# Gathering two heads in six moves, mixing and rounding on ScalarE, and a new order: a fused attention and gated feed-forward kernel

## The chip, the cores and the metric

The kernel runs on one core of one Trainium2 chip. The metric is device time in microseconds (us) of one execution. Engines are called PE (TensorE, the matrix engine), DVE (VectorE), ACT (ScalarE), POOL (GpSimd) and SP (SyncE, which issues the DMAs here).

## The reference

Inputs are q, k, v and a complex decay a of shape (4 batches, 8 heads, 768 steps, 48), and weights for a feed-forward part. In attention each head keeps a complex 48x48 state that is multiplied by the decay at every step and takes up one outer product:

```python
mag = np.sqrt(a_re * a_re + a_im * a_im)
scale = np.minimum(mag, 0.999) / (mag + 1e-06)
for t in range(S):
    new_re = ar * S_re - ai * S_im
    new_im = ar * S_im + ai * S_re
    S_re, S_im = (new_re + kv, new_im)          # kv = outer(k_t, v_t)
    y[:, :, t] = np.einsum('bhd,bhde->bhe', q[:, :, t], S_re)
```

The result, x of shape (4, 768, 384), goes through the feed-forward part:

```python
xk = mu_k * x + (1.0 - mu_k) * x_prev           # x_prev: x one step earlier
xr = mu_r * x + (1.0 - mu_r) * x_prev
k = np.maximum(xk @ w_k, 0.0)
v = k * k @ w_v                                 # 384 -> 1024 -> 384
return 1.0 / (1.0 + np.exp(-(xr @ w_r))) * v
```

## The kernel before

**Units.** The work is cut into eight units of 384 steps (half a batch each), numbered u. A unit has three parts. `gate(u)` loads q, k and a into the tile g (three column tiles ct of 128 rows), takes logarithms and angles of the decay (Ln, Exp, Arctan on ACT, prefix sums by scans on DVE), and multiplies k and q by growth and phase, which leaves cosine and sine products in g (line 777, six instructions in unit 0, two long ones later). `attend(u)` makes the attention from them: transposes `tr` of the keys, copies `kt` by ACT, state increments `up`, scores `sc`, masks `pt` by DVE, states added up by DVE, and values `y`. `mix(u)` is the feed-forward part: mixed inputs x, first products `z`, relu r, square h, second products `o`.

**Heads in pairs.** A column tile ct holds two heads in rows 0 to 47 and 64 to 111, and 16 rows of heads 6 and 7 in rows 48 to 63 and 112 to 127 of each of the three tiles. So heads 0 to 5 (pairs 0 to 2) can be scored from g as it lies, and heads 6 and 7 (pair 3) can't: their parts must be brought together by DMA. Line 806 (`move` in `stack`) does that for pair 3 with 12 moves of 16 rows, cosine and sine apart, into the tile q23. It also moves the queries of pairs 0 to 2 into the tiles q01 and q23, four moves for each pair, for the product with the state. For pair 3 both q and k go, and its scores are taken from q23 (line 986) and not from g (line 991).

**Unit 0 of the feed-forward part** uses whole fp32 weights (`wx`) and inputs; each block of weights comes as 64-bit numbers (`raw`, ten loads, 768 KB each and one of 384 KB) and is converted by ACT (line 583) and DVE (lines 586, 589, 593). From unit 1 on the weights are split into a rounded high part and a rest (`split`, lines 613 and 616), and so are x (lines 418 and 421) and h (hhi by a cast of line 495, hlo by a subtraction of line 499); every product is then three fp32r multiplications. Unit 0's x is one difference dx on DVE (line 395) and two fused multiply-adds (line 404) for each ct; it needs the rows of pair 3 back in place, which six DMAs xt<-ys do (line 1079).

**Order.** Everything is recorded as operations with reads, writes and buffer slots. A planner (`Plan.run`) plays them through with estimated costs, picking on each engine the ready operation with the lowest number of the table `ORDER`, and then emits the instructions in that order. `ORDER` holds a number for each engine of each step: "g" gate, "f" load of weights, "w" conversion, "a" attention, "m" feed-forward, "s" split. Engines run their own queues in order and wait for each other by semaphores. A DMA takes one of eight semaphores in turn, and waits until the DMA that had it eight issues earlier has landed; so at most eight are in flight from SP.

**Loads.** Those of unit 0's and unit 1's g (12 of 384 KB), the weights, and v (192 KB each) all go out from SP in the first 25 us, in the order that the table gives.

Of the kernel before, what the change touches and what calls it, by code (L numbers as in the profile page):

```python
# [22 lines left out]
P = 128  # L23
# [29 lines left out]
    ("g", 4): dict(SP=(69, 89, 43, 39, 47, 54,), ACT=(170, 75, 186, 162, 178,), DVE=(196, 188, 101, 194, 213,)),
    ("g", 5): dict(SP=(103, 102, 100, 97, 71, 81,), ACT=(148, 217, 190, 204, 206,), DVE=(154, 209, 211, 189, 172,)),
    ("g", 6): dict(SP=(105, 91, 109, 30, 107, 104,), ACT=(198, 153, 133, 211, 141,), DVE=(191, 71, 208, 179, 205,)),
    ("g", 7): dict(SP=(98, 93, 96, 94, 90, 99,), ACT=(183, 164, 201, 205, 215,), DVE=(167, 160, 171, 169, 150,)),
    ("f", 0): dict(SP=(16,)),
    ("f", 1): dict(SP=(35,)),
    ("f", 2): dict(SP=(15,)),
    ("f", 3): dict(SP=(14,)),  # L60
    ("f", 4): dict(SP=(65,)),
    ("f", 5): dict(SP=(73,)),
    ("f", 6): dict(SP=(101,)),
    ("f", 7): dict(SP=(75,)),
    ("f", 8): dict(SP=(40,)),
    ("f", 9): dict(SP=(72,)),
    ("w", 0): dict(ACT=(63,), DVE=(164,)),
    ("w", 1): dict(ACT=(120,), DVE=(142,)),
    ("w", 2): dict(ACT=(91,), DVE=(121,)),
    ("w", 3): dict(ACT=(8,), DVE=(20,)),  # L70
    ("w", 4): dict(ACT=(173,), DVE=(214,)),
    ("w", 5): dict(ACT=(60,), DVE=(138,)),
    ("w", 6): dict(ACT=(43,), DVE=(98,)),
    ("w", 7): dict(ACT=(13,), DVE=(31,)),
    ("w", 8): dict(ACT=(104,), DVE=(68,)),
    ("w", 9): dict(ACT=(9,), DVE=(56,)),
    ("a", 0): dict(DVE=(5, 6, 60, 46, 45, 42, 8, 43, 19,), SP=(12, 45, 5, 28, 83,), PE=(3, 28, 32, 4, 19, 6, 8, 31, 9,
         13, 0, 5,), ACT=(4, 122, 3, 146, 37, 20, 61,), POOL=(0,)),
    ("a", 1): dict(SP=(31, 6, 23,), PE=(23, 7, 2, 1, 39, 11, 15,), DVE=(7, 2, 9, 15, 35, 13,), ACT=(89, 23, 52, 92,
         56,)),  # L80
    ("a", 2): dict(SP=(58, 22, 34,), PE=(102, 79, 70, 92, 119, 140, 108,), DVE=(30, 85, 36, 75, 112, 137,), ACT=(35,
         114, 107, 31, 22,), POOL=(3,)),
    ("a", 3): dict(SP=(11, 67, 20,), PE=(20, 33, 52, 89, 59, 68, 43,), DVE=(44, 135, 22, 32, 161, 28,), ACT=(163, 157,
         177, 175, 62,)),
    ("a", 4): dict(SP=(80, 52, 49,), PE=(65, 170, 180, 95, 22, 93, 85,), DVE=(147, 61, 190, 50, 78, 118,), ACT=(145,
         207, 187, 195, 191,), POOL=(2,)),
    ("a", 5): dict(SP=(42, 50, 63,), PE=(124, 86, 134, 49, 66, 130, 72,), DVE=(113, 153, 134, 139, 202, 141,), ACT=(185,
         155, 152, 174, 137,)),
    ("a", 6): dict(SP=(77, 92, 84,), PE=(144, 152, 178, 179, 169, 131, 129,), DVE=(170, 183, 173, 184, 168, 193,),
         ACT=(169, 189, 159, 172, 144,), POOL=(1,)),  # L90
# [7 lines left out]
    ("m", 2): dict(DVE=(97, 23, 109, 119, 105, 86, 16, 73, 62, 29, 80, 76, 11, 37,), ACT=(67, 73, 83, 109, 93, 108, 101,
         105, 33, 119, 97, 112, 95, 124, 82,), PE=(42, 91, 16, 77, 138, 17, 14, 84, 67, 40, 99, 88, 90, 94, 24, 53, 87, 27,
         78,), SP=(74, 64, 68,)),  # L100
    ("m", 3): dict(DVE=(81, 74, 82, 132, 92, 99, 122, 47, 131, 140, 69, 91, 149, 84,), ACT=(29, 84, 30, 72, 80, 111,
# [1148 lines left out]
```

## Time and profile before

| | |
|---|---|
| three runs | 440.93, 439.72, 437.56 us; median 439.72 |
| the profiled execution | 439.72 us; its span, first to last instruction, 438.0 us |
| mean granted PE clock | 0.961 of full speed |
| PE busy | 376.4 us (86%) |
| DVE, ACT busy | 341.4 us (78%), 308.6 us (70%) |
| DMA over the span | 49.72 MB |

The rest of a run beside the span, 1.7 us, lies before the first and after the last instruction. The profile counts an instruction as busy from its start to its end; neighbours on an engine overlap a little, and matmuls overlap much. A share over the whole span says little here, since the start of the program has other limits than its middle, so the stages are read one by one.

### The profile page before, as it was taken

The numbers are of one execution on the slowest core, as the hardware profiler recorded it, in microseconds if no ns is written. First come the engines' busy times: TensorE is split into PE (matmuls) and PEld (weight loads), VectorE is DVE, ScalarE is ACT, GpSimd is POOL, SyncE is SP. The second block draws the span as 40 slices with busy tenths as digits, with TensorE's granted clock in tenths as the row PEclk, the third lists the DMA queues.
The fourth block names the chain that finished last, engine by engine and source line by source line (L and its number), as shares of the span: only waits on it lengthen the run. The fifth ranks groups of instructions, "written<-read, shape, count | busy, mean of one in ns | idle before, by whom it ended". The sixth has DMA issues, their size and how long they took to land.

```text
span 438.0 us, 13423 instructions
## 1 busy us (share of the span) xinstructions
PE 376.4 (86%) x5681; PEld 336.4 (77%) x5681; DVE 341.4 (78%) x564; ACT 308.6 (70%) x595; POOL 7.1 (2%) x30
## 2 busy tenths in 40 slices
PE   0027735999997999899999999999999999999994
PEld 0016622666576998899989999999989999999993
DVE  0998789999986889978898998979998873527232
ACT  6878385978895679876995799669968741534430
POOL 4000000000000000000000000000000000000000
PEclk9998585999998999999999999999999999999998
DMA  7996270326134513404542724164210341001001
GB/s 276 415 413 165 57 258 27 75 66 257 29 75 120 217 50 81 104 30 182 148 94 72 269 49 90 55 257 112 56 57 10 80 100 57 16 0 54 2 1 62
DMA packets 23189, 49.72 MB, mean 114 GB/s; under 512 B 4945, under 2 KB 16465, under 8 KB 23121
## 3 DMA queue, kind: packets, MB, share of 16 engines
q1 hardware_dynamic: 23120, 48.78, 35.7%
q8 instruction: 47, 0.77, 0.7%
q14 instruction: 22, 0.17, 0.1%
HBM read 31.07 MB, written 4.72 MB: 82 GB/s over the span
## 4 chain that ended last, share of the span: by engine, by line
PE 60%; DVE 14%; ACT 11%; DMA 6%; issue 4%; SPq 3%; DVEq 0%; ACTq 0%
PE z L443 23%; PE o L520 17%; PE y L1028 8%; PE up L877 4%; PE sc L991 3%; SPq L806 3%; DMA q<-g 2%; DMA xt<-ys 2%; PE tr L848 2%; DVE g L777 2%; PE sc L986 2%; DVE m L715 2%; ACT sq L317 1%; PE z L439 1%; DMA v<-in_vt 1%
## 5 line engine op out<-in xcount | busy, mean ns | idle before, releaser
L443 PE MATMUL z<-x,w 128*128 128x384 f32 x693 | 132.4, 340 | 0.0
L443 PEld LDWEIGHTS z<-x,w 128*128 128x128 f32 x693 | 119.3, 188 | 1.4
L520 PE MATMUL o<-hhi,w 128*128 128x384 f32 x336 | 87.6, 342 | 0.3 <-DVE hhi L495 0.3
L520 PEld LDWEIGHTS o<-hhi,w 128*128 128x128 f32 x336 | 59.4, 188 | 1.5 <-DVE hhi L495 0.8
L520 PE MATMUL o<-hlo,w 128*128 128x384 f32 x168 | 57.0, 339 | 0.6 <-DVE hlo L499 0.6
L484 ACT ACTIVATE r<-z 128x384 f32<-128x384 f32 x64 | 31.0, 487 | 35.4 <-PE z L443 33.2
L495 DVE CAST hhi<-h 128x384 fp32r<-128x384 f32 x56 | 19.3, 354 | 34.9 <-ACT h L488 21.9
L777 DVE TENSOR_TENSOR g<-g,r 128x768 f32<-128x768 f32 (+1 forms) x24 | 41.3, 1755 | 4.9 <-ACT r L317 4.5
L439 PE MATMUL z<-x,wx 128*128 128x384 f32 x66 | 25.5, 533 | 12.9 <-DVE x L404 12.9
L317 ACT ACTIVATE sq<-m 128x1152 f32<-128x1152 f32 (+1 forms) x30 | 28.1, 966 | 9.9 <-DVE m L698 6.1
L488 ACT ACTIVATE h<-r 128x384 f32<-128x384 f32 x64 | 33.0, 526 | 0.9
L520 PEld LDWEIGHTS o<-hlo,w 128*128 128x128 f32 x168 | 31.6, 188 | 2.2 <-DVE hlo L499 2.1
L499 DVE TENSOR_TENSOR hlo<-h,hhi 128x384 fp32r<-128x384 f32 x56 | 30.4, 553 | 1.5
L908 PE MATMUL tr<-ident,g 128*128 128x128 f32 x18 | 3.6, 335 | 32.5 <-DVE g L777 30.7
L439 PEld LDWEIGHTS z<-x,wx 128*128 128x128 f32 x66 | 13.0, 206 | 22.1 <-issue 11.9
L1028 PEld LDWEIGHTS y<-q,state 112*48 112x48 f32 (+1 forms) x704 | 24.2, 138 | 7.1 <-issue 5.3
L1028 PE MATMUL y<-q,state 112*48 112x64 f32 (+1 forms) x704 | 27.1, 233 | 2.5 <-PE up L947 0.8
L314 ACT ACT_TABLE_LOAD x22 | 28.2, 1283 | 0.4
L418 ACT CAST x<-xm 128x384 fp32r<-128x384 f32 x42 | 21.0, 513 | 9.8 <-DVE xm L410 4.9
L908 PEld LDWEIGHTS tr<-ident,g 128*128 128x128 f32 x18 | 2.3, 165 | 33.2 <-issue 29.8
L1003 DVE TENSOR_TENSOR pt<-sc,mask 128x384 f32<-128x384 f32 (+1 forms) x36 | 17.0, 507 | 13.2 <-PE sc L986 8.4
L877 PEld LDWEIGHTS up<-v,kt 64*64 64x64 f32 (+1 forms) x1216 | 21.4, 127 | 7.2 <-issue 2.8
(88 smaller groups left out, 663.1 us busy)
## 6 DMA issues: line engine op xcount, KB each, us to landing
g<-in_gat SPq DMA_DIRECT2D x18, 768.0 KB, 5.8
raw<-in_w_all SPq DMA_DIRECT2D x9, 768.0 KB, 10.5
g<-in_gat SPq DMA_DIRECT2D x12, 384.0 KB, 7.9
v<-in_vt SPq DMA_DIRECT2D x24, 192.0 KB, 3.6
q<-g SPq DMA_DIRECT2D x96, 48.0 KB, 2.2
out_t<-y SPq DMA_DIRECT2D x24, 192.0 KB, 2.3
q<-g SPq DMA_DIRECT2D x28, 144.0 KB, 3.3
q<-g SPq DMA_DIRECT2D x40, 72.0 KB, 2.8
```

Of the source, the lines that this page charges most:

```text
L314: nc.scalar.add_instruction(mybir.InstLoadActFuncSet(name=nc.get_next_instruction_name(), act_func_set_id=loaded[0], engine=mybir.EngineTy ...
L317: nc.scalar.activation(out=out, in_=in_, func=func, **kw)
L418: nc.scalar.copy(out=hi[which][:, ct], in_=xm[which, ct])
L439: nc.tensor.matmul(z, lhsT=wx[s[0]][:, s[1]], rhs=hi[which][:, ct], start=ct == 0, stop=ct == NT - 1)
L443: nc.tensor.matmul(z, lhsT=wt[s[0]][:, part, s[1]], rhs=r[which][:, ct], start=n == 0, stop=n == 3 * NT - 1)
L484: nc.scalar.activation(out=t["r", j], in_=t["f", j], func=AF.Relu, scale=1.0 / W_SCALE)
L488: nc.scalar.activation(out=t["h", j], in_=t["r", j], func=AF.Square)
L499: nc.vector.tensor_tensor(out=t["lo", j], in0=t["h", j], in1=t["hi", j].bitcast(F32), op=ALU.subtract)
L520: nc.tensor.matmul(tiles["o", mt], lhsT=w, rhs=r, start=j == 0 and n == 0, stop=j == NJ - 1 and n == len(parts) - 1)
L777: nc.vector.tensor_tensor(out=g[:, d, 2 * i:2 * i + 2], in0=g[:, d, 2:4], in1=t["r"][:, 1 - i, d].unsqueeze(2).to_broadcast([P, k, 2, U]), ...
L877: nc.tensor.matmul(t["up", c, s][i * HR:(KR if i else HR), h * D:(h + 1) * D], lhsT=keys, rhs=V[u][c][r, h * D:(h + 1) * D], start=True, s ...
L1028: nc.tensor.matmul(t["y", team][s][rows, h // 2 - team[0], c], lhsT=lhsT[:, cols], rhs=rhs, start=(s, h % 2) not in begun, stop=stop)
```

## The change

- *Heads 6 and 7 of unit 0.* Instead of 12 moves of 16x768 into q23, six moves of 16x1536 (all four rows: cosine and sine of k and q at once) bring them into a tile g67 that is laid out like g. Their scores are computed from it like those of the other pairs, with 24 multiplications instead of 12 of twice the depth. Four copies on ACT then put the queries into q23.
- *Mixed input of unit 0.* ACT writes (1 - mu) times the earlier step, DVE adds mu times x in one fused operation; the difference dx is gone there. A tile mu_1 of 1 - mu is made once.
- *Rounded h.* In units 1 to 3, for every second block j, hhi is a Square of relu on ACT and no longer a cast on DVE.
- *Prologue of unit 0.* The Relu of two of the three column tiles goes to DVE (`RELU_0`), and ACT's table set 6 is loaded ahead of everything.
- *First state of each pair in unit 0.* Copied by ACT, no longer by DVE.
- *Planner.* It now knows that at most eight DMAs are in flight (`LANES`), and starts with the table "exp" loaded. All of `ORDER` is new; two of its lines stand here for all.

```diff
 ORDER = {
-    ("g", 0): dict(SP=(7, 8, 1, 10, 13, 9, 3, 2, 0,), ACT=(36, 14, 6, 27, 25, 19, 39, 28, 41, 40, 5, 11, 18, 42, 1,),
+    ("g", 0): dict(SP=(4, 20, 11, 35, 10, 21, 22, 103, 29,), ACT=(88, 48, 54, 156, 91, 218, 166, 175, 65, 197, 223, 118,
...
-HHI_ACT = set()
+HHI_ACT = {(u, j) for u in (1, 2, 3) for j in range(1, NJ, 2)}
+RELU_0 = (1, 2)
...
+    LANES = 8
...
-        table, dma, end = None, 0.0, 0.0
+        table, dma, end = "exp", 0.0, 0.0
...
+                    if e == "SP" and len(lanes) >= self.LANES and lanes[-self.LANES] + self.LATENCY > t:
+                        continue
...
+    mu_1 = keep.tile([P, 2, NT], F32, name="mu_1")
+    nc.vector.tensor_scalar(out=mu_1, in0=mu_sb, scalar1=-1.0, scalar2=1.0, op0=ALU.mult, op1=ALU.add)
...
-                def whole_one(which=which):
+                def whole_old(which=which):
                     if which not in hi:
                         hi[which] = mp["x"].tile([P, NT, 2, U], F32R, tag=("xk", "xr")[which], name="x")[:, :, 0].bitcast(F32)
+                    nc.scalar.activation(out=hi[which][:, ct], in_=X[u][:, ct, 0:U], func=AF.Copy,
+                                         scale=mu_1[:, which, ct:ct + 1])
+
+                def whole_new(which=which):
                     nc.vector.scalar_tensor_tensor(
-                        out=hi[which][:, ct], in0=d[ct], scalar=mu_sb[:, which, ct:ct + 1],
-                        in1=X[u][:, ct, 0:U], op0=ALU.mult, op1=ALU.add)
+                        out=hi[which][:, ct], in0=X[u][:, ct, 1:U + 1], scalar=mu_sb[:, which, ct:ct + 1],
+                        in1=hi[which][:, ct], op0=ALU.mult, op1=ALU.add)
...
-                if j in HHI_ACT:
-                    nc.scalar.activation(out=t["hi", j], in_=t["h", j], func=AF.Copy)
+                if (u, j) in HHI_ACT:
+                    nc.scalar.activation(out=t["hi", j], in_=t["r", j], func=AF.Square)
...
+            if (u, j) in HHI_ACT:
+                op_act(U, h_hi, reads=[("rl", u, j)], writes=[("hhi", u, j)], uses=[sr, s1])
+            else:
+                op_dve(U, h_hi, rate=2, reads=[("h", u, j)], writes=[("hhi", u, j)], uses=[sh, s1])
...
+                if u == 0 and c.start in RELU_0:
+                    op_dve(n, positive_dve, rate=2, reads=gk(c, 0), writes=kk("m", c), uses=[s_ph, s_m, s_g])
...
+                    def gather(ct, j):
+                        if "g67" not in t:
+                            t["g67"] = mp["x"].tile([P, 2 * NT, U], F32, tag="xr", name="g67")[:, :4]
+                        o = j * HR + 16 * ct
+                        nc.sync.dma_start(out=t["g67"][o:o + 16], in_=G[u][j * HR + D:j * HR + HR, ct])
+
+                    def copy(i, j):
+                        nc.scalar.copy(out=qs[1][i * HR:i * HR + D, j, 2], in_=t["g67"][j * HR:j * HR + D, 2 * i + 1])
...
-                            nc.vector.tensor_copy(new, t["up", p, s][:, c])
+                            nc.scalar.copy(out=new, in_=t["up", p, s][:, c])
...
-                                    if p == NT:
+                                    if p == NT and u:
...
-                                    g = G[u][j * HR:j * HR + D, p]
+                                    g = G[u][j * HR:j * HR + D, p] if p < NT else t["g67"][j * HR:j * HR + D]
...
         with tc.manual_schedule():
+            load_table(6)
             plan[0].run(ORDER)
```

The instructions' order changes on every engine. Three places of it matter in what follows. SP's queue around unit 0's moves stood thus before (`q_92` is q01 and `q_93` is q23; `xt<-ys` brings heads 6 and 7 back into x):

```order
L806 DMA q_92<-g 48x384 x2
L806 DMA q_93<-g 48x384 x2
L806 DMA q_92<-g 48x384 x2
L806 DMA q_93<-g 48x384 x2
L806 DMA q_93<-g 16x768 x12
L806 DMA q_92<-g 48x384 x4
L636 DMA g<-in_gat 128x1536 x3
L1079 DMA xt<-ys 16x384 x2
L643 DMA v<-in_vt 128x384 x3
L1079 DMA xt<-ys 16x384 x4
```

and stands thus now (`g_408` is g67):

```order
L585 DMA raw<-in_w_all 128x1536
L662 DMA v<-in_vt 128x384 x3
L832 DMA q_92<-g 48x384 x4
L832 DMA q_93<-g 48x384 x4
L832 DMA q_92<-g 48x384 x4
L850 DMA g_408<-g 16x1536 x6
L655 DMA g<-in_gat 128x1536 x3
L1131 DMA xt<-ys 16x384 x6
L662 DMA v<-in_vt 128x384 x3
```

24 moves have become 18, the six xt<-ys stand together, and three loads of v have moved: two of unit 0 and one of unit 1 now go out behind the weights. On DVE, the place of unit 0's mixed input was this before (`dx` the difference, `r` and `ph` phases of unit 1, `wx` a conversion):

```order
L395 TENSOR_TENSOR dx<-xt 128x384
L742 SCALAR_TENSOR_TENSOR ph<-ph,stat,zero_77 128x384
L404 SCALAR_TENSOR_TENSOR x<-dx,mu_sb,xt 128x384 x2
L751 COPY stat<-ph 128x9
L759 TENSOR_SCALAR r<-ph 128x1152
L395 TENSOR_TENSOR dx<-xt 128x384
L762 SCALAR_TENSOR_TENSOR r<-ph,r 128x1152
L395 TENSOR_TENSOR dx<-xt 128x384
L404 SCALAR_TENSOR_TENSOR x<-dx,mu_sb,xt 128x384 x4
L586 TENSOR_SCALAR wx<-wx 128x768
```

and is this now:

```order
L777 COPY stat<-ph 128x9
L785 TENSOR_SCALAR r<-ph 128x1152
L605 TENSOR_SCALAR wx<-wx 128x768
L788 SCALAR_TENSOR_TENSOR r<-ph,r 128x1152
L418 SCALAR_TENSOR_TENSOR x<-xt,mu_sb,x 128x384 x5
L608 SCALAR_TENSOR_TENSOR wx<-raw,wx 128x768
L612 SCALAR_TENSOR_TENSOR wx<-raw,wx 128x768
L803 TENSOR_TENSOR g<-g,r 128x768 x5
L708 TENSOR_TENSOR ph<-g,ph 128x1152
L1055 TENSOR_TENSOR pt<-sc,mask 128x384 x2
L803 TENSOR_TENSOR g<-g,r 128x768
L605 TENSOR_SCALAR wx<-wx 128x768
L418 SCALAR_TENSOR_TENSOR x<-xt,mu_sb,x 128x384
```

The differences are gone, five of the six fused operations stand together, and the sixth comes after unit 1's products. On PE, the first products of the split feed-forward part (z of unit 1) stood behind unit 2's values y before:

```order
L1028 MATMUL y<-pt,v 64x64 x2
L1028 MATMUL y<-pt,v 48x64 x2
L443 MATMUL z<-x,w 128x384 x18
L991 MATMUL sc<-g 64x64 x24
L986 MATMUL sc<-q_93 64x64 x12
L443 MATMUL z<-x,w 128x384 x9
```

and stand ahead of them now, the second nine after the last `up` of unit 2:

```order
L923 MATMUL up<-v,kt 48x48 x2
L894 MATMUL tr<-ident,g 128x128 x6
L1040 MATMUL sc<-g 64x64 x48
L459 MATMUL z<-x,w 128x384 x9
L923 MATMUL up<-v,kt 64x48 x2
```

Unit 2's y now comes after 18 multiplications of z.

## Rows read from the trace of the kernel before

**Rows 1.** Busy time by stage: stretch, its length, engines with instruction counts, clock, DMA, GB/s.

```profile
0.00:29.80 29.80, 0.00 (x0) 0.00 (x0) 18.72 (x39) 22.00 (x47) 4.94 (x16) 1.00 0.94 363
29.80:58.30 28.50, 22.19 (x554) 19.13 (x554) 22.46 (x51) 18.03 (x40) 0.00 (x0) 0.76 0.52 143
58.30:72.80 14.50, 1.63 (x3) 0.52 (x3) 13.02 (x19) 9.88 (x16) 0.34 (x1) 0.64 0.54 190
72.80:130.00 57.20, 56.18 (x854) 37.64 (x857) 55.03 (x74) 51.13 (x90) 0.00 (x0) 0.97 0.34 95
130.00:140.00 10.00, 7.66 (x174) 6.08 (x168) 8.85 (x17) 5.95 (x13) 0.00 (x0) 0.88 0.52 136
160.00:180.00 20.00, 18.06 (x214) 16.95 (x214) 19.61 (x33) 17.38 (x30) 0.19 (x1) 1.00 0.31 76
180.00:300.00 120.00, 119.38 (x1967) 111.99 (x1959) 104.99 (x160) 96.83 (x183) 0.49 (x1) 1.00 0.39 122
```

**Rows 2.** Timeline of ACT in the prologue: start, length, engine, line, operation.

```profile
4.64 0.52 ACT L676 ACTIVATE m<-g 128x384 f32<-128x384 f32 x1 [2.54 <-DMA g<-in_gat]
5.18 1.28 ACT L314 ACT_TABLE_LOAD   x1
6.48 0.61 ACT L317 ACTIVATE m<-m,tiny 128x384 f32<-128x384 f32 x1
...
16.95 0.51 ACT L317 ACTIVATE sq<-m 128x384 f32<-128x384 f32 x1
```

**Rows 3.** Timeline of DVE around the six products of unit 0.

```profile
28.78 5.30 DVE L777 TENSOR_TENSOR g<-g,r 128x768 f32<-128x768 f32 x6
33.99 0.56 DVE L586 TENSOR_SCALAR wx<-wx 128x768 int32<-128x768 int32 x1
...
34.99 0.95 DVE L589 SCALAR_TENSOR_TENSOR wx<-raw,wx 128x768 int32<-128x768 int32 x1
```

**Rows 4.** Timeline of PE from its first matmul to unit 0's mixing.

```profile
29.84 0.88 PE L908 MATMUL tr<-ident,g 128*128 128x128 f32 x3 [29.84 <-DVE g L777]
...
68.85 1.62 PE L439 MATMUL z<-x,wx 128*128 128x384 f32 x2 [10.57 <-DVE x L404]
72.79 5.13 PE L439 MATMUL z<-x,wx 128*128 128x384 f32 x10 [2.32 <-DVE x L404]
```

**Rows 5.** Timeline of SP's queue, unit 0: the moves, then the gather.

```profile
29.81 20.81 SPq L806 DMA_DIRECT2D q<-g  x24
...
61.95 5.46 SPq L1079 DMA_DIRECT2D xt<-ys  x4
```

**Rows 6.** Line 806's moves over the whole run: issue in ns (min/median/max), and landing.

```profile
L806 SPq DMA_DIRECT2D q<-g x164: 503/589/1979, 29.8 to 355.6; - x164
...
DMA to landing us min/median/max: 2.1/2.6/8.5
```

**Rows 7.** Timelines of ACT, then DVE, between unit 0's values and its mixing.

```profile
57.45 0.32 ACT L1063 ACTIVATE ys<-y 112x192 f32<-112x192 f32 x1
...
64.70 0.33 ACT L1063 ACTIVATE xt<-y 48x192 f32<-48x192 f32 x1
66.71 0.56 DVE L395 TENSOR_TENSOR dx<-xt 128x384 f32<-128x384 f32 x1 [1.02 <-DMA xt<-ys]
...
72.13 2.20 DVE L404 SCALAR_TENSOR_TENSOR x<-dx,mu_sb,xt 128x384 f32<-128x384 f32 x4
```

**Rows 8.** Timelines of PE at its later waits; in brackets idle time and releaser.

```profile
137.44 2.23 PE L1028 MATMUL y<-q,state 112*48 112x64 f32 x38 [0.76 <-DMA q<-g]
...
169.79 0.85 PE L848 MATMUL tr<-ident,g 128*128 128x128 f32 x6 [0.65 <-DVE g L777]
...
179.71 0.51 PE L877 MATMUL up<-v,kt 64*48 64x48 f32 x22 [1.12 <-ACT kt L854]
```

**Rows 9.** The costliest groups on the page: one cast on DVE, one square on ACT.

```profile
L495 DVE CAST hhi<-h 128x384 fp32r<-128x384 f32 x56 | 19.3, 354 | 34.9 <-ACT h L488 21.9
L488 ACT ACTIVATE h<-r 128x384 f32<-128x384 f32 x64 | 33.0, 526 | 0.9
```

More of the change, by code (lines that the diff above doesn't have):

```diff
@@ L53 @@
[L53 to L90, printed above, removed]
@@ L98 @@
[L98 to L101, printed above, removed]
-         110, 121, 90, 81, 65, 78, 48, 10, 79,), PE=(62, 75, 69, 128, 58, 54, 73, 150, 120, 76, 61, 111, 109, 41, 107, 123,
-         57, 96, 21,), SP=(36, 51, 60,)),
@@ new lines @@
+    ("g", 6): dict(SP=(89, 96, 68, 86, 102, 97,), ACT=(186, 219, 210, 215, 216,), DVE=(209, 199, 207, 223, 217,)),
+    ("g", 7): dict(SP=(111, 104, 92, 110, 91, 112,), ACT=(211, 201, 217, 184, 153,), DVE=(140, 201, 179, 198, 210,)),
+    ("f", 0): dict(SP=(28,)),
+    ("f", 1): dict(SP=(19,)),
+    ("f", 2): dict(SP=(67,)),
+    ("f", 3): dict(SP=(40,)),
+    ("f", 4): dict(SP=(24,)),
+    ("f", 5): dict(SP=(64,)),
+    ("f", 6): dict(SP=(42,)),
+    ("f", 7): dict(SP=(83,)),
+    ("f", 8): dict(SP=(52,)),
@@ new lines @@
+    ("f", 9): dict(SP=(58,)),
+    ("w", 0): dict(ACT=(101,), DVE=(144,)),
+    ("w", 1): dict(ACT=(57,), DVE=(131,)),
+    ("w", 2): dict(ACT=(32,), DVE=(38,)),
+    ("w", 3): dict(ACT=(51,), DVE=(39,)),
+    ("w", 4): dict(ACT=(191,), DVE=(211,)),
+    ("w", 5): dict(ACT=(62,), DVE=(79,)),
+    ("w", 6): dict(ACT=(107,), DVE=(31,)),
+    ("w", 7): dict(ACT=(22,), DVE=(33,)),
+    ("w", 8): dict(ACT=(71,), DVE=(63,)),
+    ("w", 9): dict(ACT=(7,), DVE=(4,)),
+    ("a", 0): dict(DVE=(76, 138, 36, 148, 12, 46, 43, 196, 121,), SP=(9, 3, 6, 47, 13,), PE=(36, 25, 8, 18, 6, 26, 122,
+         5, 47, 13, 16, 39,), ACT=(4, 105, 28, 2, 19, 3, 15, 39, 17,), POOL=(0,)),
@@ new lines @@
+    ("m", 7): dict(DVE=(100, 80, 66, 67, 104, 113, 78, 85, 101, 88, 86, 97, 115, 93,), ACT=(108, 70, 77, 119, 106, 80,
+         95, 104, 102, 103, 83, 122, 94, 112, 127,), PE=(70, 71, 94, 72, 84, 66, 67, 76, 83, 48, 86, 100, 73, 85, 75, 93,
+         121, 53, 78,), SP=(45, 48, 43,)),
+    ("s", 0): dict(ACT=(56,), DVE=(9,)),
+    ("s", 1): dict(ACT=(23,), DVE=(44,)),
+    ("s", 2): dict(ACT=(152,), DVE=(187,)),
+    ("s", 3): dict(ACT=(209,), DVE=(216,)),
+    ("s", 4): dict(ACT=(96,), DVE=(50,)),
@@ L126 @@
+    ("s", 5): dict(ACT=(113,), DVE=(204,)),
+    ("s", 6): dict(ACT=(21,), DVE=(181,)),
+    ("s", 7): dict(ACT=(129,), DVE=(125,)),
+    ("s", 8): dict(ACT=(11,), DVE=(127,)),
+    ("s", 9): dict(ACT=(123,), DVE=(30,)),
 }
@@ L212, in run @@
         tables = sorted(o["table"] for o in ops if o["table"])[::-1]
-        table, dma, end = None, 0.0, 0.0
+        table, dma, end = "exp", 0.0, 0.0
         work = {}
         free, held, got = {}, dict.fromkeys(self.bufs, 0), dict.fromkeys(self.bufs, 0)
-        taken, waiting, events, ends, order = set(), {}, [self.BEGIN], [], []
+        lanes = [self.BEGIN + 2.5]
+        taken, waiting, events, ends, order = set(), {}, [self.BEGIN, lanes[0] + self.LATENCY], [], []
         def wait(i):
@@ L266, in run @@
                         end = dma + self.ARRIVE
+                        lanes.append(end)
                     else:
```

126 lines of the change are left out of this document (78 added, 48 removed).

## The prediction

> **What bounds the kernel now.** I read the table of busy time by stage first [rows 1], then the timelines of the engines in the stages where TensorE (PE) is not full. From 180 to 300 us PE is busy for 119.4 of 120 us at full clock. PE does the same multiplications before and after but for 24 small ones, so what can be gained is the time in which it waits. There are four such places. Until 29.84 it has nothing: its first transposes wait for the products of line 777 [rows 4]. From 29.8 to 58.3 it is busy for 22.2 of 28.5 us at a mean granted clock of 0.76. From 58.28 to 72.79 it does almost nothing: 10.57 us of wait, 1.62 us of work, 2.32 us of wait, all for unit 0's mixed input x on DVE [rows 1, 4]. Later it loses 2.3 us between 130 and 140 and 1.9 us between 160 and 180 [rows 1].
>
> **The change part by part.** The sum goes against the profiled execution, 439.72 us (span 438.0 and 1.7 around it); it is also the median of the three runs.
>
> *Prologue.* Before, ACT does the first Relu at 4.64, loads a table at 5.18 for 1.28 us, and then runs almost without a gap to 17.46 [rows 2]. The new program loads set 6 ahead of the data, so the Ln follows the Relu; two of the three Relus (0.52 each, about 0.42 net by my estimate, since neighbours overlap a little) go to DVE. This chain ends 1.28 + 0.84 = 2.1 us earlier. DVE gets the two (about 0.3 each), and order puts a second weight conversion, 0.56 + 0.95 + 0.95 = 2.5 us, ahead of the six products [rows 3]. DVE was full there, so the products end at 34.08 - 2.1 + 0.6 + 2.5 = 35.1 instead of 34.08. PE now begins with pair 0, whose product is the fifth of six (0.88 each): it starts at about 34.2, 4.4 us later than before. So up to here the change costs time. The converted block is one that DVE need not do later.
> The Trainium skill (ScalarE: Activation LUTs, What ACT_TABLE_LOAD costs) gives a table switch 1.28 us for the load and 1.38 us more for a drain. The trace shows the Ln at 6.48, right behind the load's end at 6.46, so no drain is seen; by the page the sum below would be 1.4 us lower.
>
> *Scores of heads 6 and 7.* Before, 24 moves of q (line 806) fill SP from 29.81 to 50.62, the last land near 50 [rows 5], and pair 3's scores wait for them. Now 12 moves serve pairs 0 to 2 and six gather heads 6 and 7. From 30.7 (first product) 18 issues at the median of 0.59 us [rows 6], with some 2 us of waits for the loads in flight, end at 43.5; with the median landing of 2.6 the last is there at 46, with the longest, 8.5, at 52 [rows 6]. How a 16x1536 move lands no row shows: I take the median, and either end stays hidden, because PE is then still at the pairs before. The last values v are now loaded behind all weights: 12.8 MB at 363 GB/s [rows 1] are there at about 35 us, before PE needs them. From 34.2 PE has the same 22.2 us of work, less 1 if it runs closer together and the clock rises sooner, more 3 for its waits on kt copies and masks: pair 3's values end near 58, its copies to ys at about 58.7, against 57.77 before [rows 7]. Four copies into q (0.42 each) and four of the state on ACT fall into its idle time: 18.0 of 28.5 us busy [rows 1].
>
> *Gather of x and mixing.* Before, the last four xt<-ys stand behind three loads of v on SP (the order shows it) and go from 61.95 to 67.41 [rows 5]; three differences and six fused operations on DVE follow between other work, the last needed one ending at 74.33 [rows 7]. Now the six moves stand together: 58.7 + 6 x 0.6 + 2.6 = 64.9. ACT does the table load, an arctan, one conversion and the four copies of y (before until 65.0, [rows 7]) in some 5.3 us (1.28, 1.1, 0.8 and 2.1), to 64.0, and then five scaled copies by 0.42, to 67.0; DVE follows with four fused operations, of which PE needs the third or fourth: 68.4 instead of 72.79 for the dense stretch. Gain 4.4. If copies and DVE alternate badly it is 2, if ys comes at 57.5 it is 6.
>
> *Between 72.8 and 130.* PE idles 1.0 us here [rows 1]. DVE (55.0 of 57.2 busy) has one conversion and three differences less to do. I take 0.5.
>
> *Between 130 and 140.* Unit 2's values wait for the state and then 0.76 for the q moves [rows 8], and run partly at half clock. Order now puts 9 + 9 multiplications of z (1.56 us each nine) before them. Idle 2.34 and some 1.2 us of low clock go, 3.5 in all; I take 3.0. If the store of unit 0's y, which now stands before the last four q moves on SP, comes late, nothing is gained.
>
> *Between 160 and 180.* Two waits of 0.65 and 1.12 us [rows 8], for unit 3's products and its kt copy, of 1.94 idle. DVE is full there (19.6 of 20). In units 1 to 3 twelve casts of h (0.354 us on DVE) become squares on ACT (0.526) [rows 9], and unit 3's preparation begins earlier. I take 1.5; between 0 and 1.9.
>
> *New waits* of an order that has not run: -1.0, between 0 and -5.
> Sum: 4.4 + 0.5 + 3.0 + 1.5 - 1.0 = 8.4, so 439.7 - 8.4 = 431.3.
>
> **Rivals.** (1) The start gains nothing. PE begins at 34.2 instead of 29.84, on a cold clock, and v comes last: if loads run slower than 363 GB/s or ys comes 4 us late, z starts at 72.8 as before. For it: the first multiplication waits for the fifth product, and DVE is full. Against it: the gather is shorter by six issues and undivided. Time: 439.7 - 4.0 = 435.7.
> (2) The start gains, the later waits stay or are replaced: 439.7 - 4.4 = 435.3, and with 2 us of new waits 437. For it: DVE and ACT are 96% and 89% busy from 72.8 to 130. Against it: what leaves DVE leaves it there and after.
> (3) Slower: ScalarE becomes the bound in units 1 to 3. A square for the rounded h stands in its queue between relu and square of the next block; hlo, o and the buffer of relu wait behind it. Price: the square alone 0.526 x 12 = 6.3 us; with the next block's square behind it, another 0.526 each, 12.6. From 0.7 us for each cast it eats the gain; at 1.05 the time is 431.3 + 12.6 = 443.9, with the next relu as well 450. For it: ACT is busy 96.8 of 120 us between 180 and 300. Against it: 23 us are free there, and 12 x 0.526 over units 1 to 3 is 6.3. The Trainium skill (ScalarE: Activation LUTs, Rules for kernel authors) has cheap elementwise work on VectorE rather than ScalarE, which speaks for this rival; the two durations agree with it, but they weigh only where ACT is the last to arrive.
> (4) It does more: start 6, 1.0, 3.5 and 1.9, no new waits: 427.3.
> That the six moves would not shorten the chain is part of (1).
>
> **How the numbers follow.** Forecast 0.65, with a range of its own of 427.5 to 435; (1) 0.12, (2) 0.10, (3) 0.05, (4) 0.08. The predicted time is 431.3. The range, 426.0 to 437.0, holds the forecast, (1), (2) and most of (4). A change of 1% (4.4 us) is about what a measurement of this kernel can tell: faster by more, under 435.3: 0.65 + 0.08 and half of (1) and a little of (2), 0.80. Within: 0.15. Slower, over 444.1: 0.05.
>
> **What would show it.** Right: one table load before the first Ln, Ln right behind the Relu; PE's first transpose near 34; 18 moves ending near 43; ys near 58 to 59; six xt<-ys in a row; dense z from about 68; no wait of PE over 0.7 us between 125 and 180. Wrong: z not before 72; PE waiting for hhi of line 509 or for relu; a wait of y for q behind the stores; or PE busy in fewer than 19 of 20 us anywhere between 140 and 430.

## The result and the profile after

The changed kernel takes 431.57 us (median of six, 430.48 to 434.07), the kernel before 439.75 (median of six, 437.21 to 441.0): a ratio of 0.9833, interval 0.98 to 0.9866, 8.2 us less. Timed twice more, six times each, it has medians of 430.42 and 432.45; all 18 times have their median at 431.36 and reach from 429.15 to 434.07. The profiled execution is the slowest of them, 434.07 (span 432.4), so the two traces differ by 5.65 us only, and part of the question is where the other 2.5 are.

Busy time by stage, of the kernel after, in the columns of [rows 1]:

```profile
29.80:58.30 28.50, 17.12 (x538) 14.77 (x538) 25.85 (x52) 25.76 (x54) 0.00 (x0) 0.94 0.58 165
58.30:72.80 14.50, 7.74 (x49) 4.47 (x50) 13.61 (x21) 12.54 (x21) 0.64 (x1) 0.53 0.43 153
72.80:130.00 57.20, 55.76 (x889) 37.92 (x888) 53.61 (x76) 51.11 (x98) 0.00 (x0) 1.00 0.36 103
130.00:140.00 10.00, 7.23 (x142) 6.38 (x144) 7.69 (x12) 6.29 (x11) 0.00 (x0) 0.87 0.37 91
160.00:180.00 20.00, 19.95 (x238) 19.18 (x237) 18.61 (x29) 18.52 (x35) 0.00 (x0) 1.00 0.34 76
```

Read against [rows 1]: ACT's load between 29.8 and 58.3 rose from 18.0 to 25.8 us; PE does 7.74 us of work instead of 1.63 between 58.3 and 72.8, and is full between 160 and 180 (19.95 for 18.06). Between 130 and 140 nothing is better: 7.23 for 7.66.

The start, as PE's timeline has it (its rows with a wait, in brackets):

```profile
34.98 2.15 PE L954 MATMUL tr<-ident,g 128*128 128x128 f32 x9 [34.98 <-DMA v<-in_vt]
...
48.53 0.94 PE L1080 MATMUL y<-q,state 112*64 112x64 f32 x16 [1.87 <-ACT sq L324]
...
59.41 1.09 PE L1080 MATMUL y<-q,state 112*64 112x64 f32 x16 [2.59 <-DVE state L1006]
...
66.11 1.65 PE L455 MATMUL z<-x,wx 128*128 128x384 f32 x2 [4.77 <-DVE x L418]
68.64 5.46 PE L455 MATMUL z<-x,wx 128*128 128x384 f32 x10 [0.88 <-DVE x L418]
```

PE starts 5.1 us later than before [rows 4] and still reaches the dense z at 68.64 instead of 72.79. The twelve z that were at 68.85 to 77.92 before end at 74.10.

What lies between the end of these twelve z and PE's last matmul is the same work in both kernels. One row each, over just this stretch: before, after, and the second profile of the changed kernel (experiment a1_again, 430.64 us).

```profile
77.92:431.66 353.74, 347.50 (x5115) 314.14 (x5115) 281.50 (x448) 253.69 (x490) 1.79 (x13) 1.00 0.30 89
```

```profile
74.10:426.34 352.24, 346.24 (x5115) 313.47 (x5115) 275.07 (x433) 259.19 (x503) 3.41 (x13) 1.00 0.30 89
```

```profile
73.99:423.09 349.10, 344.63 (x5116) 312.02 (x5115) 274.98 (x433) 259.24 (x503) 3.43 (x13) 1.00 0.31 90
```

PE's idle time in it (length less busy time) is 6.24, 6.00 and 4.47 us. So in the profiled pair, 3.8 us come from the start (77.92 to 74.10), 0.2 from waits, 1.3 from matmuls that stand closer together (busy 347.50 to 346.24; the increments `up` alone go from 23.9 to 22.9 us, with a mean of 217 ns for one in both), and 0.3 from the tail behind the last matmul (6.36 to 6.03): 5.6 of 5.65. In the second profile the start gives 3.9, the waits 1.8, busy time 2.9 and the tail 0.5: 9.1 us. The start is the same in both; the 3.4 us by which the two profiles differ lie behind it, nearly all at one place.

That place is in front of unit 2's values. SP's queue and PE, of the kernel after:

```profile
116.53 9.80 SPq L832 DMA_DIRECT2D q<-g  x14
126.43 2.34 SPq L560 DMA_DIRECT2D out_t<-y  x2
128.82 1.15 SPq L832 DMA_DIRECT2D q<-g  x2
130.07 0.54 SPq L560 DMA_DIRECT2D out_t<-y  x1
130.65 4.02 SPq L832 DMA_DIRECT2D q<-g  x4
```

```profile
132.43 1.84 PE L459 MATMUL z<-x,w 128*128 128x384 f32 x9
136.80 0.30 PE L1080 MATMUL y<-q,state 112*64 112x64 f32 x2 [2.53 <-DMA q<-g]
```

The nine z that the new order put ahead of y end at 134.27; the last four moves of q are issued only until 134.67, behind three stores of unit 0's result, and y waits until they land.

### The profile page after: what moved, and what is told of

The parts are those of the page before. It is cut to its first block, busy times and chain, and to the rows that moved or that the text cites. A ratio compares the mean times of both kernels' runs of the same rounds, so it can differ in the third digit from the quotient of the medians.

```text
span 432.4 us, 13450 instructions
## 1 busy us (share of the span) xinstructions
PE 372.4 (86%) x5705; PEld 333.2 (77%) x5705; DVE 338.0 (78%) x548; ACT 318.3 (74%) x618; POOL 9.0 (2%) x30
## 4 chain that ended last, share of the span: by engine, by line
PE 59%; ACT 16%; DMA 11%; DVE 8%; SPq 3%; issue 2%; ACTq 0%
PE z L459 23%; PE o L539 16%; PE y L1080 8%; DMA g<-in_gat 5%; PE sc L1040 3%; PE up L923 3%; PE z L455 3%; DMA v<-in_vt 3%; ACT r L324 2%; DMA q<-g 2%; PE tr L894 2%; SPq L832 2%; DMA xt<-ys 2%; PE sc L1035 1%; ACT sq L324 1%
## 5 line engine op out<-in xcount | busy, mean ns | idle before, releaser
L511 DVE CAST hhi<-h 128x384 fp32r<-128x384 f32 x44 | 15.5, 354 | 31.4 <-ACT h L504 17.7
L455 PE MATMUL z<-x,wx 128*128 128x384 f32 x66 | 25.8, 539 | 5.7 <-DVE x L418 5.7
L1115 ACT ACTIVATE xt<-y 112x192 f32<-112x192 f32 (+2 forms) x36 | 14.2, 396 | 19.4 <-PE y L1080 11.7
L1040 PEld LDWEIGHTS sc<-g 48*64 48x64 f32 x1200 | 22.4, 137 | 6.0 <-issue 3.4
```

Of the source, the lines that this page charges most:

```text
L455: nc.tensor.matmul(z, lhsT=wx[s[0]][:, s[1]], rhs=hi[which][:, ct], start=ct == 0, stop=ct == NT - 1)
L1040: nc.tensor.matmul(y, lhsT=g[:, 2 * i, q], rhs=g[:, 2 * i + 1, q], start=i == 0, stop=i == 1)
```

## The experiments

All are the changed kernel with one edit. Where the planner's choice would have moved other things, the edit was made behind it, so that every other instruction keeps its place. Operations are named by number in the shifts: 339, 341, 343 are the stores of unit 0; 588 to 591, 606 and 607 unit 2's last q moves.

**a1_again**: no edit.

> The changed kernel once more, nothing edited. Its six times lie between 430.48 and 434.07, and the profiled execution was the highest, 434.07 (span 432.4). Theory: most of its 2.5 us above the median come from one stretch, the wait of 2.53 us in front of unit 2's values at 136.8; then a second profile near 431.5 has that wait under 1 us and unit 0's dense z again at 68.6. Rival: the wait is in every execution, and the times vary elsewhere (loads at the start, clock): then a second profile near 431.5 has the wait at 2 to 3 us again, and z or the first transpose moved by 1 to 2 us.

Measured: 430.42 us (429.15 to 431.99). The second profile, 430.64:

```profile
130.04 3.13 SPq L832 DMA_DIRECT2D q<-g  x4
```

```profile
135.08 0.30 PE L1080 MATMUL y<-q,state 112*64 112x64 f32 x2 [1.01 <-DVE m L724]
```

The same queue, with its last four issues in 3.13 instead of 4.02 us; the wait is 1.01 instead of 2.53 (the profile names DVE's m as releaser, which ended just then; that the moves decide is shown by the next run). The starts of PE's rows up to the first split z (129.40 here, 129.60 there) agree within about 0.2 us. The theory holds, with 1.01 for its "under 1": the wait carries the difference, and a second thing goes with it. The granted clock behind it, from 137.5 to 140.9 us, is 0.50 in the first profile and 1.00 in this one:

```profile
137.50:140.90 3.40, 3.40 (x86) 3.19 (x83) 0.37 (x1) 0.00 (x0) 0.00 (x0) 0.50 0.02 5
```

```profile
137.50:140.90 3.40, 3.40 (x38) 3.33 (x29) 0.96 (x2) 2.59 (x6) 0.00 (x0) 1.00 0.00 0
```

At half clock 3.4 us hold 1.7 us of work, so by this estimate the drop costs as much as the longer wait: 1.5 + 1.7 = 3.2 of the 3.4 us between the two profiles.

**a2_stores_behind**: the stores leave their place among the moves.

```diff
+        for what, ahead, behind in SHIFTS if places else ():
+            order = [i for i in order if i not in what]
+            n = order.index(ahead) if behind is None else order.index(behind) + 1
+            order[n:n] = what
...
+SHIFTS = [([606, 607, 588, 589, 590, 591], 339, None)]
```

> The three stores of unit 0's result are taken from between unit 2's q moves on SP and put behind them; nothing else changes. Theory: the stores hold up the last moves, which are issued from 130.65 to 134.67 and land at 136.8 while PE waits 2.53 us; without them the moves are out 3 to 3.9 us earlier, unit 2's values start at about 134.3, right behind z, and the time falls by 2.5 us, with the 1.2 us of low clock up to 3.5: 428.1 to 429.1. Rival 1: something else is late next (the state sums on DVE, masks): less than 1 us, 430.6 to 431.6. Rival 2: the buffers of the result come free later and the first relus of unit 1 wait for them: as now or up to 1 us slower.

Measured: 430.08 us, 429.57 to 430.79.

```profile
116.36 14.18 SPq L832 DMA_DIRECT2D q<-g  x20
130.63 2.42 SPq L560 DMA_DIRECT2D out_t<-y  x3
```

```profile
134.02 1.38 PE L1080 MATMUL y<-q,state 112*64 112x64 f32 x40
```

The moves are out at 130.54, and y starts behind z without a wait and at full clock. The mechanism is as the theory has it; the size is not. Against the changed kernel on the same chip the median falls by 0.3 us only (430.42 to 430.08), which the six times of each don't tell apart. The one profile there has the short wait; that the other five had it too is likely, but not shown. The spread is 1.2 us over six times, against 2.8 to 3.6 in each six of the changed kernel. That it fell because of the stores is not shown either: a4_mix_on_dve, with the stores in their old place, has 1.5.

**a3_hhi_on_dve**: `h_hi` of line 509 is a `tensor_copy` of h again.

```diff
-                    nc.scalar.activation(out=t["hi", j], in_=t["r", j], func=AF.Square)
+                    nc.vector.tensor_copy(t["hi", j], t["h", j])
```

> The 12 squares of line 509 on ACT become casts on DVE again, each at the same place of the program; order as in the changed kernel. Theory of the prediction: relief of DVE is part of what took away the waits at 160 to 180 us, so 0.5 to 1.9 us come back: 432.1 to 433.5. Rival: those waits went with the order alone (unit 3's preparation earlier): 431.3 to 431.9. Second rival: the squares held up ACT, then it is faster, under 431.

Measured: 430.02 us, 429.15 to 432.4, with 430.42 for the changed kernel on the same chip. PE's waits of 140 to 400 us (us in total, times, the longest):

```profile
PE o L539 <- DVE hlo L515: 0.8, 1, 0.8
PE sc L1040 <- ACT zr L479: 0.3, 1, 0.3
```

The waits at 160 to 180 do not come back with the casts. So the squares on ACT bring and cost nothing that six times can tell; what took these waits away is the rest of the change, by argument its order, which no run put back.

**a4_mix_on_dve**: unit 0's x again from dx.

```diff
-                    nc.scalar.activation(out=hi[which][:, ct], in_=X[u][:, ct, 0:U], func=AF.Copy,
-                                         scale=mu_1[:, which, ct:ct + 1])
+                    if ct not in d:
+                        delta()
...
-                        out=hi[which][:, ct], in0=X[u][:, ct, 1:U + 1], scalar=mu_sb[:, which, ct:ct + 1],
-                        in1=hi[which][:, ct], op0=ALU.mult, op1=ALU.add)
+                        out=hi[which][:, ct], in0=d[ct], scalar=mu_sb[:, which, ct:ct + 1],
+                        in1=X[u][:, ct, 0:U], op0=ALU.mult, op1=ALU.add)
```

> Unit 0's mixed input again by three differences and six fused operations on DVE, none on ACT; order as in the changed kernel. Theory: the six moves xt<-ys land at 64.8; from there DVE has three differences (0.56), r (1.35) and four fused operations (0.57) before the x that PE needs, some 5.3 us, against 3.9 now: dense z at 70.0 instead of 68.6, 433.0. Rival: ACT's scaled copies are as slow as the differences were, and the gain came from the earlier landing alone: dense z within 0.4 of 68.6, 431.2 to 432.0.

Measured: 431.7 us, 430.64 to 432.18.

```profile
67.95 1.62 PE L455 MATMUL z<-x,wx 128*128 128x384 f32 x2 [6.39 <-DVE x L418]
69.92 5.10 PE L455 MATMUL z<-x,wx 128*128 128x384 f32 x10 [0.35 <-DVE x L418]
```

Dense z at 69.92, the twelve end at 75.02 instead of 73.99, and the median is 1.3 us above that of the changed kernel on this chip. The theory holds, with 1.3 us at dense z for its 1.4. Both numbers have an error: the six times of the two kernels overlap, and dense z starts anywhere from 67.89 (c2) to 68.64 in profiles of programs that are equal up to there (see the last section), which would make it 1.3 to 2.1.

**b1_gather_in_12** and **c3_gather_in_12_again**: the gather in halves, twice as many moves.

```diff
-                        nc.sync.dma_start(out=t["g67"][o:o + 16], in_=G[u][j * HR + D:j * HR + HR, ct])
+                        for i in (0, 2): nc.sync.dma_start(out=t["g67"][o:o + 16, i:i + 2], in_=G[u][j * HR + D:j * HR + HR, ct, i:i + 2])
```

> Heads 6 and 7 of unit 0 gathered by 12 moves of half the size (cosine and sine apart) instead of six; all else as in the changed kernel. Theory: the six more issues (0.6 to 0.7 us each) put the last one at about 49.5 instead of 45.7 and its landing at 52 to 52.5; the copies on ACT wait for it until then (now from 49.5) and pair 3's scores, now at 52.2, come 1 to 3 us later, and with them ys, the six moves and dense z: 432.5 to 434.5. Rival: the gather was hidden in any case behind PE's other pairs: within 0.5 of the changed kernel.

Measured: 431.19 us (eight times, 430.47 to 436.71), but with a profiled execution of 436.71, where pair 3's scores wait 1.73 us for the gather and dense z is at 71.45. So it was run again beside the changed kernel.

> The gather in 12 moves again, now beside the changed kernel on one chip. Before: eight times from 430.47 to 436.71, median 431.19, the profiled one the highest, with pair 3's scores waiting 1.73 us for the moves and dense z at 71.45. Theory: they are as late in every execution, and PE has it back later where it would have waited anyway, so the median is 1 to 3 us above the changed kernel's of this call. Rival: the profiled one was a rare late landing; a profile near 431 has dense z at 68 to 69 and the median is within 0.6 of the changed kernel's.

Measured: 431.71 us (429.36 to 432.69), the changed kernel 432.45 on the same chip. Profile at 431.53:

```profile
41.88 8.15 SPq L850 DMA_DIRECT2D g<-g  x12
...
58.65 3.68 SPq L1131 DMA_DIRECT2D xt<-ys  x6
```

```profile
67.17 6.59 PE L455 MATMUL z<-x,wx 128*128 128x384 f32 x12 [5.50 <-DVE x L418]
```

The six more issues are seen (8.15 us for 12, 3.76 for six in the kernel after), they end at 50.03 and the moves xt<-ys start 1 us later, but the twelve z end at 73.76, no later than in the changed kernel. Part of that is the clock: here they run without a second wait, and from 59.0 to 72.6 the mean granted clock is 0.62 where it was 0.50. In the median the rival holds: six moves instead of 12 gain nothing that is measured. But two of the 14 times with 12 moves, 436.71 and 434.79, lie above all 18 of the changed kernel, and in the one that was profiled the late moves cost 2.8 us at dense z (71.45 for 68.64). Whether six moves spare such executions, 14 times don't decide, eight of them on a chip where the changed kernel was not timed.

**c4_v_loads_between**: two moves xt<-ys, three loads of v, four moves, as before the change (`SHIFTS = [([144, 145, 367], None, 278), ([271, 272, 273, 274], None, 367)]`).

> Unit 0's six moves xt<-ys are parted again by three loads of v, as in the kernel before (two moves, three loads, four moves); all else as in the changed kernel. Theory: the loads wait for buffers that unit 0's values free at about 61.3, so the last four moves go out from 63.2 to 65.8 and land at 68.5 instead of 64.5; x and dense z come 3.5 to 4 us later, and the time is 434 to 435. Rival: x waits for DVE, which is full until 65.5 in any case: 1 to 2 us, 432 to 433.

Measured: 432.24 us (430.58 to 432.43), the changed kernel 432.45.

```profile
60.72 1.29 SPq L662 DMA_DIRECT2D v<-in_vt  x3
62.05 2.74 SPq L1131 DMA_DIRECT2D xt<-ys  x4
```

```profile
66.92 6.15 PE L455 MATMUL z<-x,wx 128*128 128x384 f32 x12 [5.84 <-DVE x L418]
```

Both sides expected a cost; none is measured. The loads wait little (60.72), and the twelve z end at 73.07, again with a mean clock of 0.62. So in the new order it gains nothing that the moves stand together. What parting them cost in the kernel before is not answered by this: there the four moves behind the loads were issued in 5.46 us [rows 5], here in 2.74.

**b2_prologue_on_act**: no `load_table(6)` ahead, and `positive_dve` is a Relu on ACT.

> Table set 6 is no longer loaded ahead, and all three Relus of unit 0 are on ACT again; all else as in the changed kernel. Theory: ACT's chain to the decay ends 1.28 to 2.1 us later, the six products and all behind them too, and since every step from there to dense z waits for the one before, the time is 432.8 to 433.7. Rival: DVE is the bound in the prologue (it has 0.36 less twice), and the chain has slack: within 0.6 of the changed kernel.

Measured: 433.35 us, 431.13 to 435.81.

```profile
36.37 2.15 PE L954 MATMUL tr<-ident,g 128*128 128x128 f32 x9 [36.37 <-DVE g L803]
...
50.10 0.65 PE L1080 MATMUL y<-q,state 112*64 112x64 f32 x16 [2.05 <-ACT sq L324]
```

The first transposes come 1.39 us later and unit 0's values 1.57 (50.10 for 48.53); the median is 2.0 us above the 431.36 of all times of the changed kernel. Those were not taken on this chip (the kernel before takes 439.71 here, 440.24 and 440.5 on the chips of the other runs), and the wait before unit 2's values (1.97 in this profile) may hold a part. The theory holds at its lower end.

**b3_conversion_behind**: `SHIFTS = [([102, 103, 104], None, 78)]`, the second conversion behind the six products.

> On DVE the second weight conversion (0.53 + 0.95 + 0.95 us), which stands among unit 0's angles and ahead of the six products, is put behind the products; all else as in the changed kernel. Theory: the conversion delays the products, as the prediction had it; now they end 2.3 us earlier, PE's first transpose is at 32.6 instead of 35.0, and dense z and the end come 1.5 to 2.3 us earlier: 429.3 to 430.1. Rival: what PE gains at the first transposes it waits for later (v landing at 35, masks and states behind the conversion on DVE): within 0.6 of the changed kernel.

Measured: 431.04 us, 430.23 to 432.37. PE, then ACT:

```profile
33.15 2.15 PE L954 MATMUL tr<-ident,g 128*128 128x128 f32 x9 [33.15 <-DVE g L803]
...
48.65 0.79 PE L1080 MATMUL y<-q,state 112*64 112x64 f32 x16 [1.84 <-ACT sq L324]
```

```profile
36.60 0.89 ACT L602 ACTIVATE wx<-raw 128x768 f32<-128x768 f32 x1 [1.68 <-DVE wx L612]
```

PE starts 1.8 us earlier and reaches unit 0's values at 48.65, where they were (48.53). The third conversion is written by ACT into the buffer of the second one's raw data, so ACT now waits 1.68 us for the second to end, and the copies of the keys and unit 1's preparation stand behind it in its queue. The rival holds: what PE gains at its first transposes it does not keep.

**b4_states_first**: `SHIFTS = [([152], None, 199), ([163, 164, 165], None, 244)]`.

> On DVE four operations of unit 1's preparation (one of 1.36 us, three of 0.95) are put behind the state sums of unit 0's pairs that they now stand between; all else as in the changed kernel. Theory: PE waits 1.87 us at 48.5 and 2.59 us at 59.4 for these sums; the first wait shrinks by 1.3 us, ys and the six moves come that much earlier, and dense z at 67.3: 430.3. The second wait shrinks too but is not on the chain, which goes over the six moves. Rival: the delayed preparation makes unit 1's products late, whose transposes already wait 0.36 us at 79.2: within 0.5 of the changed kernel.

Measured: 433.05 us. This edit changes what is computed: two operations of ACT (153 and 154) read m, and now do so ahead of 152, which writes it, so the decay of unit 1 is another one and ACT no longer waits there. What its time would be with the work intact is not known. It shows one thing that does not hang on m: ahead of 152, the ten sums still start at 47.44 (47.15 in the kernel after), waiting for ACT's copy of the first state, and PE's values follow at 48.83. So at this place there was nothing to gain.

**c1_after_third**: no edit.

> The changed kernel a third time, to stand beside the three others of this chip. 12 times so far lie between 429.15 and 434.07; two profiles had the wait in front of unit 2's values at 2.53 us (time 434.07, low clock behind it for 3.4 us) and at 1.01 (430.64, no low clock). Theory: times and this wait go together, so a profile near 431 has a wait near 1.5 and one above 433 one of 2 or more with the low clock. Rival: the times move with something else; then the wait is again 1 to 2.5 whatever the time.

Measured: 432.45 us, 430.62 to 433.39; the profile, at 433.31, has the wait again:

```profile
136.33 0.30 PE L1080 MATMUL y<-q,state 112*64 112x64 f32 x2 [1.90 <-DMA q<-g]
```

and its clock from 137.5 to 140.9 is 0.50. The three profiles agree with the theory, with 1.90 a little under its "2 or more": 2.53 us with the low clock at 434.07, 1.90 with it at 433.31, 1.01 without it at 430.64.

**c2_stores_states_hlo**: the stores behind the moves, and two of the waits that the new order brought taken out (`SHIFTS` of a2 and `([342, 343, 490, 359], None, 628), ([1488], None, 1487)`).

> Stores of unit 0 behind the q moves (as in a2_stores_behind, 430.08), and two waits that the new order brought are taken out: the four state sums of unit 2 at 125.3 on DVE stand in a row (PE waits 0.24 and 0.49 for them), and unit 6's last hlo stands right behind its hhi (PE waits 0.85 at 390.3). Theory: PE is full from 75 to 400 us, so each of the 1.6 us comes off the end: 428.5. Rival: what was put behind is late next (x of unit 1 for z at 129.4, x of unit 7 for z at 391.6): 429.5 to 430.5.

Measured: 428.9 us, 428.43 to 429.93; ratio to the kernel before 0.9762, interval 0.9717 to 0.9806. On the same chip the changed kernel takes 432.45.

```profile
300.00:400.00 100.00, 99.96 (x1411) 94.65 (x1410) 67.97 (x125) 58.85 (x126) 2.60 (x11) 1.00 0.20 52
```

```profile
73.39:420.99 347.60, 344.81 (x5116) 311.99 (x5115) 275.33 (x433) 259.29 (x503) 3.40 (x13) 1.00 0.31 90
```

From the end of the twelve z to the last matmul PE is idle for 2.79 us, where it was 6.00. The theory's 428.5 holds to 0.4 us. This version beats both kernels (no time of it reaches the lowest of the changed kernel on this chip, 430.62), and its six times lie within 1.5 us. In its profile 0.7 us come from the start and not from the edits: the twelve z end at 73.39 for 74.10, with a second wait of 0.18 for 0.88.

## Why the prediction was right, and where it was not

The forecast was 431.3 and the measured median 431.57, by a gain of 8.2 for 8.4. Its main step, the start, came out nearly as worked out. Of the later steps one failed in a part of the executions, others were too large, and gains that nobody forecast made up for them; that the sum comes within 0.3 us is partly luck.

*The start, 4.4 us.* Dense z at 68.64 for 68.4 predicted, from 72.79: 4.15, and 3.8 at the end of the twelve. The steps at its end hold: the moves of pair 3's values begin at 57.59 for 58.7, they have landed at 64.76, when ACT goes on with x, for 64.9, and ACT's five copies end at 67.40 for 67.0:

```profile
64.76 2.64 ACT L414 ACTIVATE x<-xt,mu 128x384 f32<-128x384 f32 x5 [1.25 <-DMA xt<-ys]
```

As forecast, next to nothing of the 4.15 is gained ahead of these moves: they begin at 57.59, where the first two began at 57.88 before. But the term for PE's work up to there ("22.2 us of work, less 1", "more 3" of waits) is right by luck: from 34.98 to 56.84 PE is busy for 17.12 us and waits for 4.74, and 1.9 us of unit 0's work comes later. Before, up to 57.13, it was busy for 21.04 us and waited for 6.3. So PE starts 5.1 us later and makes it up by 3.9 us less busy time and 1.5 us less waiting. The busy time is mostly a matter of the clock. Before, it was at 0.50 from 38.6 to 42.0 and from 45.5 to 55.6 us, with PE busy for 11.4 us; now it is from 48.7 to 52.1. By these rows the half clock cost about 5.7 us before and 1.7 now (an estimate). Nor did PE start "on a cold clock", as rival (1) has it: the granted clock was 1.00 from 34.98 to 48.6.

All but 0.3 us, then, is gained between the moves and z. Before, the last four moves were out at 67.41, DVE began the mixing at 66.71, and PE's dense z followed 6.08 us later [rows 4, 5, 7]. Now the moves are out at 61.86, DVE begins at 65.45, and it takes 3.19 us:

```profile
65.45 1.14 DVE L418 SCALAR_TENSOR_TENSOR x<-xt,mu_sb,x 128x384 f32<-128x384 f32 x2
67.44 1.68 DVE L418 SCALAR_TENSOR_TENSOR x<-xt,mu_sb,x 128x384 f32<-128x384 f32 x3 [0.85 <-ACT x L414]
```

Of the reasons given against rival (1), that the gather is "shorter by six issues" gains nothing in the median (c3), and that the moves stand together gains nothing in the new order (c4). The mixing on ACT is worth 1.3 us (a4), and the prologue's edits are worth 1.4 us at the first transposes (b2). The rest agrees with the order of DVE's queue: unit 1's phases ph and r, some 3 us of work, stood between the differences and now stand ahead of x. That is read from the rows; no run put them back.

*The prologue.* ACT's chain was to end 2.1 us earlier, the products at 35.1.

```profile
0.82 1.28 ACT L317 ACT_TABLE_LOAD   x1 [0.82 <-PEq L1292]
4.53 0.52 ACT L695 ACTIVATE m<-g 128x384 f32<-128x384 f32 x1 [2.43 <-DMA g<-in_gat]
5.15 0.61 ACT L324 ACTIVATE m<-m,tiny 128x384 f32<-128x384 f32 x1
```

```profile
30.07 5.87 DVE L803 TENSOR_TENSOR g<-g,r 128x768 f32<-128x768 f32 x6
```

The first Ln follows the Relu 1.33 us earlier than in [rows 2], and the products end at 35.94, 0.84 later than worked out; PE's first transpose is at 34.98 for 34.2. The term was mis-sized: undone, it costs 1.4 and not 2.1. That fits an early load that counts in full and Relus (0.84) that do not reach the chain; b2 undid both at once, so the two were not parted. The Trainium skill (ScalarE: Activation LUTs, What ACT_TABLE_LOAD costs) would have the early load save a drain of 1.38 us as well. The 1.39 us for all the prologue's edits leave no room for it, if what ACT saves reaches PE, and the trace again shows no drain: the Ln stands right behind the Relu, at 5.15. That the second conversion "costs time" ahead of the products is right for PE's first transposes and wrong for the end (b3): ACT hides it, which has to wait for this conversion in any case.

*Between 72.8 and 130, 0.5 us.* It became a loss of 0.4: idle 1.44 for 1.02 [rows 1]. DVE has less to do, but the new order stands a result, an x and a split between the state sums for which PE waits. That is the third row here, of PE's waits from 76 us on in the kernel after (engine, line and tile waited for: us in total, times, the longest):

```profile
PE y L1080 <- DMA q<-g: 2.8, 2, 2.5
PE o L539 <- DVE hlo L515: 0.8, 1, 0.8
PE sc L1040 <- DVE state L933: 0.7, 2, 0.5
```

*Between 130 and 140, 3.0 us.* This is the step that failed in the profiled execution: idle there is 2.77 us, more than the 2.34 before, and the low clock is still there (0.87 for 0.88). The z did move ahead of y. The condition put beside the term, that nothing is gained if the stores ahead of the last four q moves come late, is what happened, and a wait of y for q behind the stores stood among the signs of a wrong step. It should have been weighed with the queue's own rows, of the kernel before:

```profile
120.46 13.82 SPq L806 DMA_DIRECT2D q<-g  x20
134.38 1.75 SPq L541 DMA_DIRECT2D out_t<-y  x3
```

From 116.5 on, 13.82 and 1.75 us end at 132.1 and land at about 134, just where the z end (134.27). So there was no slack at all, and the 23 issues then took 18.1 us, the last four alone 4.02. One of these four took 2.07 us (1.16 in a1) and the other three 0.6 each; what held that one was not taken apart. In the profile of a1 (430.64) the idle time is 1.27 and there is no low clock, and the term is there to the greater part: 1.1 + 1.7 = 2.8. That it comes and goes carries the difference between the three profiles of this program; that it also spreads the other 15 of the 18 times over 4.9 us is likely, but not shown.

*Between 160 and 180, 1.5 us.* Right in size (1.94 idle became 0.53 between 160 and 185, with the wait of 0.48 for zr in it), wrong in part of its cause: it is not DVE's relief by the squares (a3); the order is what is left.

*New waits, 1.0 us.* There are two of some size, 0.73 for the state sums, which is in the -0.4 above, and 0.85 for an hlo at 390. In the profile of a1 the terms behind the start then come to -0.4 + 2.8 + 1.4 - 0.85 = 2.95 us, where 4.0 were forecast (0.5 + 3.0 + 1.5 - 1.0); in the first profile they come to -0.3. What made up for it was not foreseen: the same 5115 matmuls take 1.3 us less because they stand closer together, the tail is 0.3 to 0.5 us shorter, and the median lies between the two profiles.

*The rivals.* (1), that the start gains nothing, is out by 3.8 us. (2), that the later waits stay or are replaced, is near the profiled execution (434.07 for 435.3), and out for the median. (3), ScalarE as the bound, is out: with the squares taken away from ACT the time is the same (430.02 and 430.42), and PE's waits have no row for an hhi of line 509. The rule of the Trainium skill named there (ScalarE: Activation LUTs, Rules for kernel authors), cheap work on VectorE, makes no difference here in either direction, since there, but for the 0.48 us of zr, neither engine is the last to arrive. (4), 427.3, lies below all 18 times (the lowest is 429.15); c2, with the waits edited out, comes to 428.9.

*The signs.* The Ln behind the Relu, the first transpose near 34, the six xt<-ys in a row and z from about 68 came as named. The 18 moves ended at 45.70 and not near 43, since the first 12 took 10.80 us; PE did not wait for them. The wait of 2.53 us breaks the sign of no wait over 0.7 between 125 and 180.

## What to carry to other kernels

A move of work ahead of a wait pays only as far as the thing waited for is in time: look at the queue that brings it, and at every transfer in it that nobody waits for, such as a store of a finished result. Putting three stores behind 20 moves cost nothing that was measured and took away a wait of 1.0 to 2.5 us and, where it came, the low clock behind it. And an edit that speeds the start of a chain shows its worth only where the chain ends: 1.8 us at the first matmul were worth nothing at unit 0's values (b3), and a start that came 5.1 us later cost nothing there either.

## What was not expected of the hardware

A wait of PE can cost more than its length. Behind 2.53 and 1.90 us at this place the granted clock was 0.50 for 3.4 us, which is another 1.7 us; behind 1.01 it was 1.00. It is no matter of length alone: in c4_v_loads_between the same wait was 1.92 us and in b2_prologue_on_act 1.97, and the clock stayed at 1.00 (c4's row of 137.5 to 140.9 us below), while in b1_gather_in_12 1.71 us were followed by 0.50 from 139.7 to 143.1. And the issue of the same four moves behind the same stores took 4.02, 4.08 and 3.13 us in the three profiles of one program; the two longer ones are those with the low clock, but c4 has 4.02 too, without it.

```profile
137.50:140.90 3.40, 3.40 (x76) 3.25 (x72) 0.34 (x1) 2.02 (x5) 0.00 (x0) 1.00 0.03 5
```

Likewise a short wait can cost more than itself under unit 0's first z. In the changed kernel the half clock lasts until 72.6 us. In a3_hhi_on_dve, with no edit ahead of this place, the moves xt<-ys landed 0.8 us earlier (ACT goes on with x at 63.96 for 64.76); the twelve z begin at 66.20 (66.11), run without the second wait of 0.88 us, and the half clock ends earlier (59.0 to 72.6 has a mean of 0.62 instead of 0.50). They end at 72.44 instead of 74.10. By these rows about half of the 1.66 us is the wait and half the clock. So 1.7 us of a single profile's start can be chance, and a step is better read where an engine begins than where its matmuls end.
